# Attention, routed experts and an MLP on one core: scatters, slots and the masks of the block factors in another order

## The chip, the core and the metric

The kernel runs on one core of a Trainium2 chip. The core has five engines with a queue of instructions each, executed in the order of the program: TensorE (PE) for matmuls, VectorE (DVE), ScalarE (ACT), GpSimd (POOL) and SyncE (SP), which here only issues transfers. The metric is the time of one execution on the device in microseconds (us).

## The reference

Three layers follow each other. The first is a recurrent attention with gates, over 4 batches, 8 heads, 768 tokens and a head width of 40; the second sends each of the 3072 tokens to one of 8 experts; the third is a gated MLP.

```python
for t in range(S):                                  # attention
    m_new = max(f_gate[t] + m, i_gate[t])
    f_stab, i_stab = exp(f_gate[t] + m - m_new), exp(i_gate[t] - m_new)
    C = f_stab * C + i_stab * outer(v[t], k[t])
    n = f_stab * n + i_stab * k[t]
    y[t] = sigmoid(o_gate[t]) * (C @ q[t]) / max(abs(n @ q[t]), 1)
...
idx = argmax(norm(x) @ norm(expert_emb).T / tau)    # experts
out[idx == e] = gate * (relu(x[idx == e] @ w1[e]) @ w2[e])
...
h = x @ w_in                                        # MLP
return (h * sigmoid(1.702 * h)) @ w_out
```

## The kernel before

The attention works in 24 units, one for each batch and each chunk of 128 tokens, chunk by chunk: unit u is batch u mod 4 of chunk u // 4. One loop (`for u in range(0, NU - 1)`) writes out by hand what stands where: inside `tc.manual_schedule()` every engine gets its instructions in the order of the text, so an instruction that waits holds all behind it on its engine. Iteration u holds pieces of several units at once:

- TensorE: `scores_mm(u)` (sp, L483), `route_rank` every fourth time (L668 to L672), `pv(u - 1)` (op, L546), `route_t(u - 2)` (the transposes pr of x, L590 to L592), `state(u)` (dC, L497), `inter(u)` (ip, L533), `far_mm(u + 1)` (tri, L439), `route_l(u - 2)` (the router's products, L621 to L623, into a PSUM bank r that is there once).
- VectorE: `state_up(u - 1)` (Cst, L518), `epilogue1` (num, L558), `scan(u + 1)` (tri from fb, L427; pmb, L431, in the first two chunks), `route_slot` (L689, L691), `scores_w(u)` (wm, L488), halves of expert weights (L110, L111, L121), `epilogue2` (L565 to L574), the copy of the router's result out of bank r (logit_all, L625), `route_hot` (L643 to L651) and `route_cnt` (L680, L681) for four tiles at a time.
- ScalarE: the copy of the scan's half block (pmb, L429), `rk_all` (L674), the ones of vp_in (L464), xT (L594), the sigmoid (L552), the squares (L600), `state_decay(u)` (L504) and `far_out(u + 1)` (pmb, L444).
- GpSimd: `finish(u - 2)` (sg, L581, and x, L584), `vprime(u + 1)` (vp_in, L463), `kweigh(u + 1)` (kw, L470), and from iteration 10 on `scatter` (L699), an indirect transfer that puts one tile of x into the experts' rows, with a small memset behind it.
- SyncE: the loads of k, q, v and of the decays fb for later units, and of expert weights.

From chunk 2 on (unit 8 and later) the decays of a chunk between its two halves are a product of two factors. `factors` makes fb in iteration 4. `suffix` makes facA on VectorE in two parts (L360, iterations 5 and 6), and its second part also casts it to fa on ScalarE (L364) and subtracts on VectorE (L366). `spread_b` makes eight masked copies of fb on ScalarE (rhsB, L382), `spread_a` four of fa (lhsA, L378); `far_mm` multiplies them, and `far_out` copies the result into pmb. In iteration 6 two tiles are routed, 3 and 4, one after the other. The slots that `route_slot` finds are what the scatters of the tiles need; `route_hot` runs at the end of iterations 6, 9, 13, 17 and 21, rank and slots in the next.

Of the kernel before, what the change touches and what calls it, by code (L numbers as in the profile page):

```python
# [26 lines left out]
def kernel(ctx, tc, qT_in, kT_in, kvo_in, i_gate, f_gate, expert_emb, tau, w12, wio, out, dbg=None):  # L27

    nc = tc.nc
    B, H, S = i_gate.shape  # L30
# [110 lines left out]
    with ExitStack() as actx:  # L141
# [11 lines left out]
        R3, HP, CH = 3 * BH, P // 2, 2  # L153
# [16 lines left out]
        units = [(b, c) for c in range(NCH) for b in range(B)]  # L170
# [182 lines left out]
        def suffix(second):  # L353

            if not second:
                nc.gpsimd.memset(facA[:, :, HP - 1:HP], 1.0)
                nc.gpsimd.tensor_copy(facA[:, :, 0:HP - 1], fz[:, CH:NCH, 1:HP])
            k = 8 if second else 1
            while k < (HP if second else 8):
                nc.vector.tensor_tensor(out=facA[:, :, 0:HP - k], in0=facA[:, :, 0:HP - k], in1=facA[:, :, k:HP], op=ALU.mult)  # L360
                k *= 2
            if not second:
                return
            nc.scalar.copy(fac["fa"], facA)  # L364
            lo = slice(BH, 2 * BH)
            nc.vector.tensor_tensor(out=fac["fa"][lo], in0=facA[lo], in1=fac["fa"][lo].bitcast(F32), op=ALU.subtract)  # L366
# [75 lines left out]
        def far_out(u):  # L442
            if units[u][1] >= CH:
                nc.scalar.copy(pm[u][:, :, HP:P], tri_t.pop(u))  # L444
# [21 lines left out]
        def kweigh(u, eng=nc.gpsimd):  # L466
            if units[u][1] == NCH - 1:
                return
            kw[u] = wk.tile([P, H, D], F32, tag="kw", name="kw")
            eng.tensor_tensor(out=kw[u], in0=kvo[u][:, 0],  # L470
                                    in1=pm[u][:, :, P - 1:P].to_broadcast([P, H, D]), op=ALU.mult)
# [13 lines left out]
        def scores_w(u):  # L485
            wm[u] = wk.tile([P, H, P], F32, tag="wm", name="wm")
            for hs, sp in sp_t.pop(u):
                nc.vector.tensor_tensor(out=wm[u][:, hs], in0=sp, in1=pm[u][:, hs], op=ALU.mult)  # L488
# [173 lines left out]
        def route_rank(us, late=None):  # L662

            oh, old, new = hot[us[0]]
            rp = r_bank(late)
            n = len(us)
            rk = rp[:, 0:n * E].rearrange("p (n e) -> p n e", e=E)
            nc.tensor.matmul(rk, ones16, base16.unsqueeze(1).to_broadcast([P, n, E]), start=True, stop=False)  # L668
            nc.tensor.matmul(rk, ones16, old.unsqueeze(1).to_broadcast([P, n, E]), start=False, stop=False)
            for i in range(n - 1):  # L670
                nc.tensor.matmul(rk[:, i + 1:n], ones16, oh[:, i:i + 1].to_broadcast([P, n - 1 - i, E]), start=False, stop=False)
            nc.tensor.matmul(rk, tri16, oh, start=False, stop=True)  # L672
            if late is None:
                nc.scalar.copy(rk_all[:, tile_ids(us)], rk)  # L674
            rp_t[us[0]] = rk
# [7 lines left out]
        def route_slot(us, late=False):  # L683
            n = len(us)
            oh, old, new = hot[us[0]]
            rk = rp_t.pop(us[0])
            tis = tile_ids(us)
            sl_ = wk.tile([P, n, E], F32, tag="sl_", name="sl_")
            nc.vector.tensor_tensor(out=sl_, in0=rk, in1=oh, op=ALU.mult)  # L689
            with nc.allow_low_precision(reason="whole numbers, one of them not zero"):  # L690
                nc.vector.tensor_reduce(out=slot_i[:, tis], in_=sl_, axis=AX.X, op=ALU.add)  # L691
            if late:
                nc.vector.tensor_copy(rk_all[:, tis], rk)
# [183 lines left out]
        with tc.manual_schedule():  # L877
# [34 lines left out]
            for u in range(0, NU - 1):  # L912
                if ok(u - 4):
                    finish(u - 2, nc.gpsimd)
                if ok(u + 2):
                    fload(u + 2)
                if u == 3:
                    finish(1, nc.gpsimd)
                if u > 1:
                    scores_mm(u)  # L920
                if u > 1:
                    state_up(u - 1)
                if ok(u - 1):
                    epilogue1(u - 1)
                if u == 1:
                    state(0)
                    scores_w(1)
                    state_up(0)
                if u in (2, 5):
                    scores_w(u)  # L930
                if u and ok(u + 1):
                    scan(u + 1)
                if batch:
                    route_rank(batch)
                    route_slot(batch)
                    pend.extend(batch)
                if u not in (0, 1, 2, 5):
                    scores_w(u)
                if u == 2:
                    norm_en2()  # L940
                if u == 4:
                    gates_z(2, NCH)
                if 0 <= u - 1 - W0 < WH:
                    split_half_lo(u - 1 - W0)
                if u == 0:
                    scan(1)
                    gates_m(2, NCH)
                if ok(u - 1):
                    pv(u - 1)
                    epilogue2(u - 1)  # L950
                if u == 5:
                    gates_pe(2, NCH)
                if u in (5, 6):
                    suffix(u == 6)
                if u == 1:
                    masks()
                if ok(u + 1):
                    vprime(u + 1)
                    if units[u + 1][1] < CH:
                        kweigh(u + 1)  # L960
                if u == 3:
                    gates_x(2, NCH)
                if u == 4:
                    put_dec(1)
                    gates_exp_i(2, NCH)
                rts = {2: [], 3: [0], 4: [1], 5: [2], 6: [3, 4]}.get(u, [u - 2] if ok(u - 2) else [])
                if rts:
                    route_t(rts[0])
                if u == NU - 2:
                    inter(u + 1, True)  # L970
                if u > 4:
                    sigm(u)
                elif u < 2:
                    sigm(u + 1)
                if u == 4:
                    order_consts()
                if u == 2:
                    finish(0, nc.gpsimd)
                if u:
                    state(u)  # L980
                if u == 3:
                    prep_en()
                if len(rts) > 1:
                    route_t(rts[1])
                    route_l(rts[0])
                inter(u)
                if ok(u + 1):
                    far_mm(u + 1)
                for i in rts[-1:]:
                    route_l(i)  # L990
                for i in rts:
                    route_sq(i)
                    if i % B == B - 1:
                        newb = [i - j for j in range(B - 1, -1, -1)]
                        route_hot(newb)
                if batch:
                    route_cnt(batch)
                batch, newb = newb, None
                state_decay(u)
                if ok(u + 1) and units[u + 1][1] >= CH:  # L1000
                    far_out(u + 1)
                    kweigh(u + 1)
                if u in (5, 6):
                    spread_b(H // 2 * (u - 5), H // 2 * (u - 4))
                if u == 6:
                    spread_a()
                if u == 3:
                    sigm(u)
                    gates_exp_f(2, NCH)
                    gates_xi(2, NCH)  # L1010
                if u == 4:
                    gates_e(2, NCH)
                    sigm(u)
                for i in range(0 if u < US else 1 if u < NU - 5 else 2):
                    if pend:
                        scatter(pend.pop(0))
                if ok(u + 3):
                    load_k(u + 3)
                    load_q(u + 3)
                    load_v(u + 3)  # L1020
                if 0 <= u - Z0 < NZ:
                    zero_slots(u - Z0)
                if u == W0 - 2:
                    first()
                if u == W0 - 1:
                    ids[0] = nc.values_load(first_i, engines=[mybir.EngineType.SP], min_val=0, max_val=E - 1)
                if u in WLOAD:
                    load_w(WLOAD.index(u))
                if 0 <= u - W0 < WH:
                    split_half(u - W0)  # L1030
# [697 lines left out]
```

## Time and profile before

| | us |
|---|---|
| median of 3 runs (768.67 to 770.9) | 770.32 |
| the profiled execution | 769.16 |
| its span, first to last instruction | 767.5 |

Busy time of the engines by stretch of the span, in us, with the granted TensorE clock and the share of the DMA engines:

| stretch | TensorE | VectorE | ScalarE | GpSimd | clock | DMA |
|---|---|---|---|---|---|---|
| 0 to 74, attention, first two chunks | 52.73 | 59.87 | 32.71 | 35.10 | 0.91 | 0.72 |
| 74 to 211, attention, other chunks, end of it | 118.62 | 110.45 | 65.98 | 82.72 | 1.00 | 0.61 |
| 211 to 405, experts | 191.72 | 171.04 | 124.00 | 74.40 | 1.00 | 0.72 |
| 405 to 767.5, MLP | 353.01 | 188.29 | 144.67 | 38.53 | 0.99 | 0.14 |

A busy time is a sum over a stretch and does not tell which engine the others wait for; that is read from the rows of the waits and from the instructions in order of time. A clock of 1.00 is the full TensorE clock of 2.4 GHz, 0.50 its lower level of 1.2 GHz.

### The profile page before, as it was taken

The page shows a single profiled execution, that of the slowest core. Times are in us where ns is not written, and L with a number is a line of the kernel's source. Part 1 is how long each engine was busy: PE and PEld are TensorE (multiplying, and loading weights), DVE is VectorE, ACT ScalarE, POOL GpSimd, SP SyncE. Part 2 cuts the span into 40 slices and gives each one's busy share as a digit, 9 for nine tenths or more (in the row PEclk, how much of TensorE's full clock was granted, in tenths as well). Part 3 has the DMA queues.
Part 4 walks back from the last instruction along what each step waited for, and adds up shares of the span by engine and source line. Part 5 has one row for each costly group of instructions (what it writes and reads, how often), then busy time and mean ns, then how long its engine had stood idle before and what let it go on. Part 6 is the DMA issues. An engine that isn't in the chain of part 4 may idle for free.

```text
span 767.5 us, 13326 instructions
## 1 busy us (share of the span) xinstructions
PE 716.1 (93%) x4724; PEld 672.3 (88%) x4724; DVE 529.6 (69%) x1095; ACT 367.4 (48%) x852; POOL 230.8 (30%) x348
## 2 busy tenths in 40 slices
PE   7695988888889999999999999999999999999995
PEld 6595887888789999999999988998898889889994
DVE  7896888788569899898986764554554554445542
ACT  4354454553456666576655443343343343334442
POOL 4462456577424333364511003003003002002011
PEclk9997999999999999999999999999999999999998
DMA  6984866673268776867853121110111111101000
GB/s 188 309 254 152 261 213 195 170 236 129 88 233 208 208 220 204 193 206 238 251 143 101 22 62 35 37 47 35 36 48 35 32 31 36 43 1 44 13 18 18
DMA packets 70490, 95.78 MB, mean 125 GB/s; under 512 B 31794, under 2 KB 56530, under 8 KB 70418
## 3 DMA queue, kind: packets, MB, share of 16 engines
q1 hardware_dynamic: 67346, 86.99, 39.2%
q0 software_dynamic: 3072, 7.89, 2.8%
q8 instruction: 38, 0.62, 0.3%
q14 instruction: 34, 0.28, 0.1%
HBM read 73.73 MB, written 17.19 MB: 118 GB/s over the span
## 4 chain that ended last, share of the span: by engine, by line
issue 41%; PE 23%; POOL 5%; DVE 2%; DMA 1%; POOLq 0%; ACT 0%; SPq 0%; ACTq 0%
PE acc L1228 11%; PE hp L138 10%; POOL out_dram L1273 3%; POOL xr L1379 2%; PE xt L1152 1%; DMA xr<-y 1%; DVE w L121 0%; POOL gap L1275 0%; DVE hs L1202 0%; DVE xl L1154 0%; DVE w L111 0%; DVE fr L1297 0%; POOLq L1723 0%; DVE xl L1170 0%; PE xt L1168 0%
## 5 line engine op out<-in xcount | busy, mean ns | idle before, releaser
L1228 PE MATMUL acc<-wout,hhl 128*128 128x320 f32 x1152 | 187.0, 309 | 0.0
L1228 PEld LDWEIGHTS acc<-wout,hhl 128*128 128x128 f32 x1152 | 175.9, 188 | 7.4
L1213 DVE TENSOR_TENSOR sg<-hp,sg 128x512 f32<-128x512 f32 (+1 forms) x112 | 68.9, 615 | 93.5 <-ACT sg L1212 86.8
L138 PE MATMUL hp<-xh,win 128*128 128x512 f32 (+1 forms) x560 | 131.0, 364 | 0.0
L1212 ACT ACTIVATE sg<-hp 128x512 f32<-128x512 f32 (+1 forms) x112 | 60.4, 539 | 124.5 <-PE hp L138 124.0
L1215 DVE TENSOR_TENSOR hhl<-sg,hhl 128x512 fp32r<-128x512 f32 (+1 forms) x112 | 71.4, 637 | 70.3 <-ACT hhl L1214 69.8
L1273 POOL DMA_INDIRECT out_dram<-o,tokd x24 | 24.1, 1002 | 312.2 <-ACT o L1257 308.6
L1228 PE MATMUL acc<-w,hs 128*128 128x320 f32 x636 | 104.9, 310 | 2.0 <-ACT hs L1201 1.0
L138 PEld LDWEIGHTS hp<-xh,win 128*128 128x128 f32 x560 | 93.9, 188 | 11.5 <-ACT xh L1418 0.2
L1214 ACT CAST hhl<-sg 128x512 fp32r<-128x512 f32 (+1 forms) x112 | 62.7, 560 | 80.2 <-DVE sg L1213 75.9
L1228 PEld LDWEIGHTS acc<-w,hs 128*128 128x128 f32 x636 | 96.8, 188 | 4.5 <-DVE hs L1202 1.9
L138 PE MATMUL hp<-xl,win 128*128 128x512 f32 (+1 forms) x336 | 85.7, 363 | 0.0
L110 POOL TENSOR_TENSOR w<-r,w 128x256 fp32r<-128x256 f32 x58 | 47.7, 823 | 106.6 <-ACT w L105 90.4
L138 PEld LDWEIGHTS hp<-xl,win 128*128 128x128 f32 x336 | 58.8, 189 | 10.9 <-DVE xl L1419 0.2
L138 PE MATMUL hp<-xh,w 128*128 128x440 f32 (+6 forms) x320 | 66.8, 338 | 0.0
L483 PE MATMUL sp<-qT,kblk 120*128 120x128 f32 x384 | 50.7, 289 | 4.1 <-DVE wm L488 4.1
L138 PEld LDWEIGHTS hp<-xh,w 128*128 128x128 f32 x320 | 51.4, 189 | 1.7
L483 PEld LDWEIGHTS sp<-qT,kblk 120*128 120x128 f32 x384 | 48.5, 205 | 5.0 <-DVE wm L488 4.5
L1201 ACT ACTIVATE hs<-hp 128x440 fp32r<-128x440 f32 (+6 forms) x64 | 30.3, 473 | 41.6 <-PE hp L138 38.7
L546 PE MATMUL op<-vp_in,wm 128*128 128x96 f32 (+1 forms) x368 | 44.2, 273 | 0.1
L546 PEld LDWEIGHTS op<-vp_in,wm 128*128 128x128 f32 x368 | 42.9, 192 | 0.3 <-DVE num L565 0.3
L138 PE MATMUL hp<-xl,w 128*128 128x440 f32 (+6 forms) x192 | 42.9, 331 | 0.0
(324 smaller groups left out, 1126.4 us busy)
## 6 DMA issues: line engine op xcount, KB each, us to landing
r<-in_w_dram SPq DMA_DIRECT2D x32, 704.0 KB
kvo<-in_kvo_dram SPq DMA_DIRECT2D x24, 480.0 KB
c<-in_wio_dram SPq DMA_DIRECT2D x16, 704.0 KB
rows<-zt SPq DMA_DIRECT2D x8, 640.0 KB
qT<-in_qT_dram SPq DMA_DIRECT2D x24, 180.0 KB
fb<-dec SPq DMA_DIRECT2D x32, 128.0 KB
fb<-dec SPq DMA_DIRECT2D x7, 512.0 KB
xr<-y SPq DMA_DIRECT2D x5, 640.0 KB
```

The source lines that it names most:

```text
L110: eng.tensor_tensor(out=t[:, 3 * P:5 * P].rearrange("p (c f) -> p c f", c=2), in0=r1[:, 0:2], in1=hif[:, 0:2], op=ALU.subtract)
L138: nc.tensor.matmul(hp, a, b, start=(i == 0), stop=(i == len(seq) - 1))
L483: nc.tensor.matmul(sp[:, h - hs.start], kblk[u % NLD][0:KR, h // 3, h % 3, :], qT[u][0:KR, h // 3, :], start=True, stop=True)
L546: nc.tensor.matmul(ops[:, h * NW:h * NW + n], wm[u][:, h], vp_in[u % NLD][:, h * DV:h * DV + n], start=True, stop=True)
L1201: nc.scalar.activation(out=hh, in_=hp, func=AF.Relu)
L1212: nc.scalar.activation(out=sg, in_=hp, func=AF.Sigmoid, scale=1.702)
L1213: nc.vector.tensor_tensor(out=g, in0=hp, in1=sg, op=ALU.mult)
L1214: nc.scalar.copy(hh, g)
L1215: nc.vector.tensor_tensor(out=hl, in0=g, in1=hh.bitcast(F32), op=ALU.subtract)
L1228: nc.tensor.matmul(acc_t[blk][i], hl if j == 2 else hh, w[:, DM:2 * DM] if j == 1 else w[:, 0:DM], start=(first and j == 0), stop=(last an ...
L1273: sc = nc.gpsimd.indirect_dma_start(out=out, out_offset=bass.IndirectOffsetOnAxis(ap=tokd[:, ti:ti + 1], axis=0), in_=o[:, i], in_offset=None)
L1379: eng.tensor_tensor(out=xr_t[blk], in0=xr_t[blk], in1=gated[:, t0:t0 + n].unsqueeze(2).to_broadcast([P, n, 3 * P]), op=ALU.mult)
```

## The change

Three things in the unit loop are written in another order; no operation is added or left out. `suffix` no longer holds the cast of facA to fa and the subtraction: a new function `factor_a` holds them and is called in iteration 6 behind the decay of the state, ahead of `spread_a`. `spread_b` makes all eight copies in iteration 5 instead of four in 5 and four in 6. The scatters stand ahead of `far_out` and `kweigh`, so on GpSimd ahead of the weighing of the keys (`far_out` is ScalarE's and keeps its place there). And `route_slot` stands behind `scores_w`.

```diff
             while k < (HP if second else 8):
                 nc.vector.tensor_tensor(out=facA[:, :, 0:HP - k], in0=facA[:, :, 0:HP - k], in1=facA[:, :, k:HP], op=ALU.mult)
                 k *= 2
-            if not second:
-                return
+
+        def factor_a():
             nc.scalar.copy(fac["fa"], facA)
             lo = slice(BH, 2 * BH)
             nc.vector.tensor_tensor(out=fac["fa"][lo], in0=facA[lo], in1=fac["fa"][lo].bitcast(F32), op=ALU.subtract)
...
                 if batch:
                     route_rank(batch)
+                if u not in (0, 1, 2, 5):
+                    scores_w(u)
+                if batch:
                     route_slot(batch)
                     pend.extend(batch)
-                if u not in (0, 1, 2, 5):
-                    scores_w(u)
...
                 state_decay(u)
-                if ok(u + 1) and units[u + 1][1] >= CH:
-                    far_out(u + 1)
-                    kweigh(u + 1)
-                if u in (5, 6):
-                    spread_b(H // 2 * (u - 5), H // 2 * (u - 4))
-                if u == 6:
-                    spread_a()
...
                 for i in range(0 if u < US else 1 if u < NU - 5 else 2):
                     if pend:
                         scatter(pend.pop(0))
+                if ok(u + 1) and units[u + 1][1] >= CH:
+                    far_out(u + 1)
+                    kweigh(u + 1)
+                if u == 5:
+                    spread_b(0, H)
+                if u == 6:
+                    factor_a()
+                    spread_a()
```

ScalarE from the end of iteration 5 to the end of iteration 6, before (rhsB and lhsA are the masked copies, xT the router's input, sg a sigmoid, sq squares, Cst the state):

```order
L382 ACTIVATE rhsB<-fb,hmask 96x4x64 x4
L364 CAST fa<-facA 96x256
L464 COPY vp_in_123<-ei_tok 128x8
L594 COPY xT<-pr 128x384
L552 ACTIVATE sg<-kvo 128x320
L594 COPY xT<-pr 128x384
L600 ACTIVATE sq,ss_all<-x 128x320 x2
L504 ACTIVATE Cst_190<-Cst_190,gdec 120x123 x3
L382 ACTIVATE rhsB<-fb,hmask 96x4x64 x4
L378 ACTIVATE lhsA<-fa,bmask 96x256 x4
```

The same place on ScalarE after the change:

```order
L382 ACTIVATE rhsB<-fb,hmask 96x4x64 x8
L464 COPY vp_in_123<-ei_tok 128x8
L594 COPY xT<-pr 128x384
L552 ACTIVATE sg<-kvo 128x320
L594 COPY xT<-pr 128x384
L600 ACTIVATE sq,ss_all<-x 128x320 x2
L504 ACTIVATE Cst_190<-Cst_190,gdec 120x123 x3
L364 CAST fa<-facA 96x256
L378 ACTIVATE lhsA<-fa,bmask 96x256 x4
```

The cast has moved from ahead of both xT to behind the decay, and the second four copies of fb from behind the decay to ahead of xT.

VectorE at the end of iteration 6 and in iteration 7, where the subtraction L366 and the slots (sl_, slot_i) change places with their neighbours:

```order
 L649 TENSOR_REDUCE mx<-vv 128x4
 L651 TENSOR_TENSOR oh_all<-vv,mx 128x4x8
+L366 TENSOR_TENSOR fa<-facA,fa 32x256
 L518 SCALAR_TENSOR_TENSOR Cst_190<-dC,mask_178,Cst_190 120x3x41 x3
 L558 TENSOR_TENSOR num<-ip,ei_tok 128x328
 L427 SCALAR_TENSOR_TENSOR tri<-fb,id_132 128x512
-L689 TENSOR_TENSOR sl__840<-r,oh_all 128x32
-L691 TENSOR_REDUCE slot_i<-sl__840 128x4
 L488 TENSOR_TENSOR wm<-sp,pmb_141 128x1024
+L689 TENSOR_TENSOR sl__842<-r,oh_all 128x32
+L691 TENSOR_REDUCE slot_i<-sl__842 128x4
 L565 TENSOR_TENSOR num<-num,op 128x328
```

The subtraction now stands between the routing and the state's update, no longer directly behind facA's products, and the slots stand behind the weighing of the scores.

GpSimd in one of the iterations 10 to 18, before:

```order
L584 TENSOR_TENSOR x<-num,sg 128x320
L463 TENSOR_TENSOR vp_in_122<-kvo,ei_tok 128x8x40
L470 TENSOR_TENSOR kw<-kvo,pmb_141 128x320
L699 DMA rows<-x,slot_i 26624x320
L701 MEMSET gap 1x1
L581 TENSOR_TENSOR sg<-sg,dn 128x320
L584 TENSOR_TENSOR x<-num,sg 128x320
```

The same on GpSimd after the change:

```order
L584 TENSOR_TENSOR x<-num,sg 128x320
L463 TENSOR_TENSOR vp_in_122<-kvo,ei_tok 128x8x40
L699 DMA rows<-x,slot_i 26624x320
L701 MEMSET gap 1x1
L470 TENSOR_TENSOR kw<-kvo,pmb_141 128x320
L581 TENSOR_TENSOR sg<-sg,dn 128x320
L584 TENSOR_TENSOR x<-num,sg 128x320
```

The scatter and its memset have moved from between kw and sg to between vp_in and kw. From iteration 19 on no keys are weighed, and the order there is the same as before.

## Rows read from the trace of the kernel before

**Rows 1.** Windows: stretch, its length, busy us (instructions), granted clock, DMA share, GB/s.

```profile
60.80:67.20 6.40, 0.02 (x1) 0.00 (x0) 5.65 (x10) 0.90 (x4) 2.99 (x4) 0.63 0.12 28
67.20:73.70 6.50, 6.47 (x34) 6.47 (x35) 2.22 (x11) 6.07 (x17) 0.00 (x0) 0.58 0.37 98
73.70:80.00 6.30, 6.30 (x63) 6.24 (x63) 5.40 (x17) 3.41 (x12) 1.06 (x2) 1.00 0.77 250
```

**Rows 2.** Timeline, ScalarE: start, us, what; in brackets idle before it and releaser.

```profile
53.83 1.69 ACT L382 ACTIVATE rhsB<-fb,hmask 96x256 fp32r<-96x256 f32 x4
66.30 0.41 ACT L364 CAST fa<-facA 96x256 fp32r<-96x256 f32 x1 [10.78 <-DVE facA L360]
...
66.71 0.47 ACT L594 COPY xT<-pr 128x384 f32<-128x384 f32 x1
```

**Rows 3.** Timeline, VectorE, iterations 6 and 7.

```profile
64.23 1.98 DVE L360 TENSOR_TENSOR facA<-facA 96x224 f32<-96x224 f32 x3
66.73 0.41 DVE L366 TENSOR_TENSOR fa<-facA,fa 32x256 fp32r<-32x256 f32 x1 [0.53 <-ACT fa L364]
...
71.48 0.17 DVE L625 COPY logit_all<-r 128x8 f32<-128x8 f32 x1 [2.39 <-PE r L623]
...
72.68 0.85 DVE L518 SCALAR_TENSOR_TENSOR Cst<-dC,mask,Cst 120x123 f32<-120x123 f32 x3
```

**Rows 4.** Timeline, TensorE, iterations 6 and 7.

```profile
57.79 0.27 PE L592 MATMUL pr<-ident,x 128*128 128x128 f32 x1
...
67.23 0.80 PE L621 MATMUL r<-enT,xT 128*128 128x128 f32 x2 [6.41 <-ACT xT L594]
...
69.88 0.71 PE L621 MATMUL r<-enT,xT 128*128 128x128 f32 x2
...
71.23 2.66 PE L483 MATMUL sp<-qT,kblk 120*128 120x128 f32 x16
```

**Rows 5.** Waits from 55 to 190 us: who for whom, us in total, times, longest.

```profile
POOL kw L470 <- ACT pmb L444: 42.9, 12, 12.2
...
PE pr L590 <- POOL x L584: 12.4, 11, 1.7
```

**Rows 6.** Timeline, GpSimd: an x, four steps in a row, another scatter.

```profile
80.44 1.60 POOL L584 TENSOR_TENSOR x<-num,sg 128x320 f32<-128x320 f32 x1
...
114.37 0.74 POOL L470 TENSOR_TENSOR kw<-kvo,pmb 128x320 f32<-128x320 f32 x1 [2.66 <-ACT pmb L444]
115.27 1.82 POOL L699 DMA_INDIRECT rows<-x,slot_i  x1 [0.16 <-issue]
...
117.14 0.73 POOL L581 TENSOR_TENSOR sg<-sg,dn 128x320 f32<-128x320 f32 x1
117.95 0.88 POOL L584 TENSOR_TENSOR x<-num,sg 128x320 f32<-128x320 f32 x1
...
123.06 1.01 POOL L699 DMA_INDIRECT rows<-x,slot_i  x1 [0.15 <-issue]
```

**Rows 7.** Timeline, VectorE: two scans, and one of the five first slots.

```profile
79.95 1.50 DVE L427 TENSOR_TENSOR_SCAN tri<-fb,id 128x512 f32<-128x512 f32 x1
...
115.05 1.22 DVE L427 TENSOR_TENSOR_SCAN tri<-fb,id 128x512 f32<-128x512 f32 x1
...
126.69 0.19 DVE L689 TENSOR_TENSOR sl__1467<-r,oh_all 128x32 f32<-128x32 f32 x1 [0.73 <-ACT rk_all L674]
```

**Rows 8.** Timeline, TensorE, iterations 13 to 15: scores and the transposes behind them.

```profile
113.60 1.95 PE L483 MATMUL sp<-qT,kblk 120*128 120x128 f32 x16
...
118.88 0.33 PE L590 MATMUL pr<-ident,x 128*128 128x128 f32 x1 [1.60 <-POOL x L584]
...
121.41 1.95 PE L483 MATMUL sp<-qT,kblk 120*128 120x128 f32 x16
...
126.61 0.33 PE L590 MATMUL pr<-ident,x 128*128 128x128 f32 x1 [1.08 <-POOL x L584]
...
133.79 0.33 PE L590 MATMUL pr<-ident,x 128*128 128x128 f32 x1 [0.98 <-POOL x L584]
```

## The prediction

> **What bounds the kernel now.** The change sits in the loop over 24 units (iteration u) of the attention, so I first cut the trace into stretches. In each the reader should look at TensorE's busy time and at its granted clock. Around 61 to 67 us TensorE does next to nothing, and after that it works at a mean granted clock of 0.58, which is mostly the lower of its two levels (1.2 instead of 2.4 GHz): 34 matmuls in 6.5 us, against 63 in the 6.3 us that follow [rows 1]. That is one stall. To see what ends it I read ScalarE, VectorE and TensorE in order of time there [rows 2 to 4]. ScalarE stands 10.78 us at the cast of facA into fa (L364), because the products that make facA (L360) are late on VectorE, from 64.23 to 66.21. Behind the cast, in program order, stands the copy xT (L594), and TensorE waits 6.41 us for it.
>
> From iteration 11 to 19 there is a second loss, found in the list of waits: TensorE's transposes of x (pr, L590) wait for GpSimd's x (L584), 12.4 us in 11 waits, while GpSimd itself waits 42.9 us for pmb before it weighs keys (kw, L470) [rows 5]. GpSimd's order there is kw, scatter, sg, x [rows 6]: the scatter lies on the way from pmb to x, though it needs nothing from kw. TensorE's unit shows it: scores start at 113.60, pr at 118.88 after 1.60 us of waiting, the next scores at 121.41 [rows 8]. So 7.81 us a unit, 6.21 without the wait. In this stretch TensorE's own work is the floor, and x is what it waits for.
>
> **Part 1: the cast of fa and the masked copies.** The order on ScalarE after the change is: eight masked copies of fb at the end of iteration 5, then xT, xT, squares, decay, and only then the cast. The eight copies take twice the 1.69 us of four [rows 2], from 53.83 to 57.2. They are hidden: ScalarE was idle there until 66.30, and the first pr that it copies is finished at 58.06 [rows 4]. So the first xT (0.47 us) ends at about 58.6 instead of 67.18, and route_l of the first tile (L621) and the state's matmuls run by some 62.5 us instead of from 67.23 on.
>
> Then a new wait takes the place of the old. Both route_l write the same PSUM bank r, so the second needs VectorE's copy of the first (L625), and that copy stands in VectorE's queue behind facA's products. Until 66.21 it cannot start; with it at 66.21 to 66.4, the second route_l starts at 66.4 instead of 69.88 [rows 4]. From that start to the second copy L625 it was 71.48 - 69.88 = 1.60 us [rows 3, 4], so the copy comes at 68.0 instead of 71.48: 3.5 us sooner. The routing steps up to Cst (L518) were 72.68 - 71.48 = 1.20 us, and now the subtraction L366 (0.41 us, before it lay in a pause) stands there too: 68.0 + 1.20 + 0.41 = 69.6 against 72.68, **3.1 us** [rows 3]. TensorE's scores of unit 7 would come at 66.4 + (71.23 - 69.88) = 67.75, 3.5 us sooner; VectorE is the later one, so 3.1 counts. Behind the cast ScalarE has only the masked copies of fa, as long as four of fb, 1.69 us; they wait for L366 at 69.6 and end at 71.3, and the copy of tri behind them has to wait for the next scan anyway. SyncE's loads of q wait for the state's matmuls and go out sooner, at a time when hardly any DMA runs (a share of 0.12 [rows 1]).
>
> Bounds: TensorE now pauses some 4 us instead of 6.4, and I expect the clock to fall all the same. If the low clock lasts as long after the pause as it did, it covers half a unit more of pv than before: 2.5 us. If the clock does not fall or is back sooner, the scores are 0.7 us shorter (2.66 against 1.95 us [rows 4, 8]) and the second route_l by about 0.4: 4.2 us. I take 3.1, which leaves the clock as the rows show it.
>
> **Part 2: the scatter ahead of kw.** In iterations 10 to 18 the scatter now fills GpSimd's wait for pmb. It starts behind vp and takes 1.01 to 1.82 us [rows 6] of a wait that was 2.8 us on the mean without the longest ((42.9 - 12.2) / 11) [rows 5], so kw starts when it did. The nine pr of iterations 11 to 19 lose their scatter. Their waits are all of [rows 5] less two small ones, 11.5 us: that is the ceiling.
>
> But the scatter also met something: VectorE's scan (L427, 1.22 us) began at 115.05 and ended at 116.27 [rows 7], and the scatter beside it took 1.82 us, clear of it 1.01; an x that met the scan of 79.95 took 1.60 against 0.88 [rows 6, 7]. Now sg meets it. In iteration 13, kw ends at 115.11. If the scan holds sg until 116.27, sg ends at 117.0 (0.73), x at 117.95 (0.88 and 0.08 between), pr at 118.0 instead of 118.88: 0.87 us. If sg goes first, the scan follows and x is the long one: 115.84 + 0.08 + 1.60 = 117.52, pr at 117.57: 1.31 us. I take 1.05 for the four iterations of this kind (12, 13, 16, 17): 4.2 us. In 14 and 18 VectorE first does the routing, the scan comes later than sg and x, and the wait of 1.08 [rows 8] goes altogether: 2.15 us. In 11, 15 and 19 VectorE comes late out of the slots, its late scan holds ScalarE's copy of tri and with it xT, pmb and kw; the wait there is 0.98 [rows 8]. I take 0.2 each, 0.6, between -0.1 and 0.98. Sum 4.2 + 2.15 + 0.6 = **6.9 us**; bounds 4 x 0.87 + 2 x 0.5 - 0.3 = 4.2 and 4 x 1.31 + 2.15 + 2.95 = 10.3.
>
> The Trainium skill, page "SBUF — State Buffer", section "SBUF: two separate sides", has a rule that speaks against this part: VectorE and GpSimd share one pair of ports under an exclusive lock, a VectorE instruction with two SBUF inputs takes it against a GpSimd instruction that reads SBUF, and whoever comes second waits for the whole of the other. By it the scatter was partly paying a lock that somebody has to pay, and the four iterations give about 1 us each; without it they would give their full waits of 1.6 and the sum would be 9 us. The 1.82 and 1.60 us of the trace agree with the rule.
>
> **Part 3: slots behind the weighing of scores.** The slots (L689) waited 0.73 us for ScalarE's rk_all in each of five iterations [rows 7], and the weighing (L488) behind them; now the weighing goes first and covers that wait. VectorE gains 3.6 us in all. I cost it at nothing: TensorE waits for x, not for VectorE, and the sum of part 2 already lets VectorE run close behind. The slots read bank r later, which the next route_l needs; by the spacing above it is free just in time. Bounds: 0.3 us lost to 0.7 gained in each, within the range of part 2.
>
> **Sum.** 3.1 + 6.9 = 10.0 us; the sum of the bounds is 6.7 to 14.5. Nothing behind the attention waits on a fixed time: the experts and the second MLP follow TensorE. The profiled execution took 769.16 us, so 759.2; the median of the runs shown is 1.16 us above it, so I predict **760.3 us**, its own range 755.8 to 763.6.
>
> **Rivals.** (1) VectorE takes over. Its lateness passes through scan, tri, xT, pmb and kw into x. Then 11, 15 and 19 lose 0.5 us each, the four gain 0.5 each and 14 and 18 gain 0.6: 1.7 instead of 6.9, with part 1 together 4.8, so 765.5. For it speaks that VectorE has little slack left after slots; against, that part 3 gives it 0.73 us just there. (2) The scan does not meet sg and all nine waits go: 3.1 + 11.5 = 14.6, so 755.7. For it speaks the 6.21 us of TensorE; against, the 1.60 us x. (3) The scatter's place gives nothing, because xT becomes the later input: part 1 alone, 767.2; half of this case is a part 1 so small that no change can be told. (4) Slower: the low clock stays. TensorE's pause is cut in two, with the state's matmuls in the middle, and if the clock falls later and then does not come back, a unit of 6.2 us takes 6.2 x 63/34 = 11.5 [rows 1], 5.3 more. From two such units it eats the 10 us, three give 776. Against it speaks that after the pause TensorE has more to do without a break than before, and that the clock came back there.
>
> **How the numbers follow.** Forecast 0.60, rival 1 0.16, rival 2 0.08, rival 3 0.10, rival 4 0.06. The range goes from rival 2 to rival 1, 755.5 to 766.0, and leaves out rivals 3 and 4. A measurement tells about 0.3% (2.3 us) from no change: faster 0.60 + 0.16 + 0.08 + half of 0.10 = 0.89, same 0.05, slower 0.06.
>
> **What would show it.** Part 1: ScalarE's wait of 10.78 us at the cast is gone or harmless, xT at about 58.6, TensorE waiting for L625 until about 66.4, scores of unit 7 at 67.5 to 68. Part 2: the scatter between vp and kw, TensorE's waits for x down from 12.4 to about 5 us, long sg or x (1.5 us) beside the scan, units of 6.7 instead of 7.8 us. Part 3: no wait for rk_all. It is wrong if kw starts later behind the scatter, if TensorE then waits for xT or for bank r, or if the clock stays low past 72 us.

## The result and the profile after

The changed kernel took **757.52 us** (median of 4 runs, 756.38 to 759.28), the kernel before beside it 770.09 us: a ratio of 0.984, 95% interval 0.982 to 0.987. It was measured twice more, on two chips on which the kernel before took 766.78 and 766.77 us: 756.38 (ratio 0.987, 0.985 to 0.989) and 755.92 (0.986, 0.984 to 0.987). So the gain is 12.6 us in the first measurement and 10.4 and 10.9 in the later two; forecast were 10.0.

**Part 1 in the trace.** ScalarE around iteration 6, by start, duration, engine, line and what ended the idle time, against [rows 2]:

```profile
52.97 3.29 ACT L382 ACTIVATE rhsB<-fb,hmask 96x256 fp32r<-96x256 f32 x8
57.23 0.48 ACT L594 COPY xT<-pr 128x384 f32<-128x384 f32 x1 [0.89 <-PE pr L592]
...
65.38 0.40 ACT L364 CAST fa<-facA 96x256 fp32r<-96x256 f32 x1 [2.87 <-DVE facA L360]
```

The eight masked copies lie in one piece. xT is copied at 57.23, 9.5 us sooner than before, and the wait at the cast has gone from 10.78 us to 2.87, with nothing behind it for which TensorE then waits. The new wait is where it was forecast. TensorE, VectorE, and the time on either side of the pause (columns of the last: stretch in us; its length; busy time and instructions of TensorE, of its weight load, of VectorE, ScalarE and GpSimd; granted clock; DMA share; GB/s):

```profile
60.46 0.80 PE L533 MATMUL ip<-Cst,qT 120*128 120x123 f32 x6
65.57 0.46 PE L621 MATMUL r<-enT,xT 128*128 128x128 f32 x2 [4.31 <-DVE logit_all L625]
```
```profile
63.37 1.97 DVE L360 TENSOR_TENSOR facA<-facA 96x224 f32<-96x224 f32 x3
65.27 0.15 DVE L625 COPY logit_all<-r 128x8 f32<-128x8 f32 x1
```
```profile
61.30:65.50 4.20, 0.00 (x0) 0.00 (x0) 3.95 (x9) 1.33 (x6) 2.56 (x4) 1.00 0.71 208
65.50:71.60 6.10, 6.03 (x44) 6.00 (x45) 4.89 (x14) 2.75 (x8) 0.43 (x1) 0.72 0.47 148
71.60:77.70 6.10, 6.10 (x57) 6.02 (x55) 4.63 (x16) 2.91 (x9) 2.74 (x3) 1.00 0.53 158
```

The copy of the first logits stands behind facA's products in VectorE's queue, so the second round starts at 65.57 instead of 69.88 [rows 4]. Against [rows 1], TensorE does 44 matmuls in the 6.1 us behind the pause, at 0.72, where it did 34 at 0.58.

**Part 2 in the trace.** GpSimd in iteration 12 to 13, against [rows 6]:

```profile
105.68 1.07 POOL L699 DMA_INDIRECT rows<-x,slot_i  x1 [0.16 <-issue]
...
108.19 0.74 POOL L470 TENSOR_TENSOR kw<-kvo,pmb 128x320 f32<-128x320 f32 x1 [1.35 <-ACT pmb L444]
108.89 1.71 POOL L581 TENSOR_TENSOR sg<-sg,dn 128x320 f32<-128x320 f32 x1
110.67 0.81 POOL L584 TENSOR_TENSOR x<-num,sg 128x320 f32<-128x320 f32 x1
```

VectorE's scan beside it, and the same operations (scan, sg, x) one iteration earlier:

```profile
102.69 1.56 DVE L427 TENSOR_TENSOR_SCAN tri<-fb,id 128x512 f32<-128x512 f32 x1 [0.18 <-DMA fb<-dec]
102.44 0.72 POOL L581 TENSOR_TENSOR sg<-sg,dn 128x320 f32<-128x320 f32 x1
103.24 1.60 POOL L584 TENSOR_TENSOR x<-num,sg 128x320 f32<-128x320 f32 x1
...
108.86 1.22 DVE L427 TENSOR_TENSOR_SCAN tri<-fb,id 128x512 f32<-128x512 f32 x1
```

The scatter now lies inside the wait for pmb. What it met there, sg and x meet instead: sg takes 1.71 us beside a scan of 1.22, or, where sg comes first (at 102.44, 0.72 us), scan and x stretch to 1.56 and 1.60. Both cases that the forecast spoke of occur. The Trainium skill, page "SBUF — State Buffer", section "SBUF: two separate sides", has whoever comes second in the pair of ports shared by VectorE and GpSimd wait for the whole of the other. Here 1.71 us is the scan's rest of 1.19 (108.86 + 1.22 less 108.89) and about half a us, where a wait for the whole and then sg's 0.72 would make 1.91. So the rule's direction holds here, with some overlap. The list of waits, 50 to 180 us, against [rows 5] (who for whom, us in total, times, longest):

```profile
POOL kw L470 <- ACT pmb L444: 30.2, 12, 9.0
...
PE r L621 <- DVE logit_all L625: 4.3, 1, 4.3
PE pr L590 <- POOL x L584: 4.2, 9, 0.8
```

TensorE's wait for x fell from 12.4 us to 4.2 (forecast: about 5). No wait for rk_all is left.

**By stretches.** The starts of scores (L483, TensorE) cut the attention into units. Three stretches serve for all that follows: scores 6 to 8 (part 1), 11 to 20 (part 2), 20 to 23 (the last units).

| kernel | 6 to 8 | 11 to 20 | 20 to 23 |
|---|---|---|---|
| before | 24.47 | 68.31 | 19.11 |
| after, first measurement | 21.27 | 60.70 | 19.57 |
| after, measured again (e8_after, e9_after) | 21.87, 21.85 | 60.66, 60.95 | 19.53, 18.90 |

Of the 11.56 us between the two first profiled executions (769.16 and 757.6), 3.20 lie in the first stretch, 7.61 in the second, -0.46 in the third; 0.87 more stands at scores 6 already, ahead of anything that the change moves. Taken by its places, the forecast of 3.1 and 6.9 looks right. The experiments show that this is not all of it.

### The profile page after: what moved, and what is told of

The parts are those of the page before. It is cut to its first block, busy times and chain, and to the rows that moved or that the text cites. A ratio compares the mean times of both kernels' runs of the same rounds, so it can differ in the third digit from the quotient of the medians.

```text
span 755.9 us, 13328 instructions
## 1 busy us (share of the span) xinstructions
PE 714.8 (95%) x4724; PEld 671.3 (89%) x4724; DVE 527.7 (70%) x1095; ACT 367.3 (49%) x852; POOL 234.3 (31%) x348
## 4 chain that ended last, share of the span: by engine, by line
issue 41%; PE 24%; POOL 5%; DVE 1%; DMA 1%; POOLq 0%; ACT 0%; SPq 0%; ACTq 0%
PE acc L1230 12%; PE hp L138 11%; POOL out_dram L1275 3%; POOL xr L1381 2%; PE xt L1154 1%; DMA xr<-y 1%; POOL gap L1277 0%; DVE w L121 0%; POOLq L1725 0%; DVE xl L1172 0%; PE xt L1170 0%; DVE hs L1204 0%; DVE xl L1156 0%; DVE w L111 0%; ACT w L118 0%
## 5 line engine op out<-in xcount | busy, mean ns | idle before, releaser
L138 PEld LDWEIGHTS hp<-xl,win 128*128 128x128 f32 x336 | 58.8, 189 | 10.9 <-DVE xl L1421 0.2
L483 PE MATMUL sp<-qT,kblk 120*128 120x128 f32 x384 | 50.7, 289 | 2.6 <-DVE wm L488 2.6
L483 PEld LDWEIGHTS sp<-qT,kblk 120*128 120x128 f32 x384 | 48.2, 204 | 3.4 <-DVE wm L488 2.8
```

The costliest lines, as they stand in the source:

```text
L138: nc.tensor.matmul(hp, a, b, start=(i == 0), stop=(i == len(seq) - 1))
L483: nc.tensor.matmul(sp[:, h - hs.start], kblk[u % NLD][0:KR, h // 3, h % 3, :], qT[u][0:KR, h // 3, :], start=True, stop=True)
```

## The experiments

The experiments ran in three groups of four kernels (e1 to e4, e5 to e8, e9 to e12), each group on a chip of its own, with the kernel before timed beside it (766.88, 766.78, 766.77 us). Where two kernels of different groups are compared, the text says so.

**Each part alone, and parts 1 and 2 without 3.** e1_cast has part 1 alone: the cast of fa and its masked copies behind the state's decay (`factor_a` as in the change), and all of spread_b in iteration 5:

```diff
-                if u in (5, 6):
-                    spread_b(H // 2 * (u - 5), H // 2 * (u - 4))
+                if u == 5:
+                    spread_b(0, H)
                 if u == 6:
+                    factor_a()
                     spread_a()
```

> Only part 1 on the kernel before: the cast of fa and its subtraction behind the decay of iteration 6, all eight masked copies of fb in iteration 5. My theory: the three parts work in different stretches and add up. From the scores of unit 6 to those of unit 8 it was 24.47 us before and 21.27 with all three parts; part 1 alone gives this whole 3.2 us, and the units from 10 to 20 stay at 68.3 us: 770.1 - 3.2 = 766.9. Rival: the low clock eats part 1 (the scores of unit 7 took 3.48 us in the changed kernel), so in another execution it gives between 2 and 4: 766 to 768. If it gives less than 1, the 3.2 came from elsewhere.

e2_scatter moves only far_out and kweigh behind the scatters:

```diff
-                if ok(u + 1) and units[u + 1][1] >= CH:
-                    far_out(u + 1)
-                    kweigh(u + 1)
...
                     if pend:
                         scatter(pend.pop(0))
+                if ok(u + 1) and units[u + 1][1] >= CH:
+                    far_out(u + 1)
+                    kweigh(u + 1)
```

> Only part 2 on the kernel before: scatters ahead of the weighing of the keys. My theory: this is the larger half. From the scores of unit 11 to those of unit 20 it was 68.31 us before and 60.70 with all parts; part 2 alone gives 6 to 7.6 of it: 762.5 to 764. Waits of TensorE for x go from 12.4 us to about 4 to 6, and sg or x beside the scan are long (1.6 to 1.7 us). Rival: the slots in the old place make VectorE too late in iterations 10, 14 and 18, and part 2 without part 3 gives 5 or less: 765 or more. Other rival, no lock: all of 11.5 us, 758.6.

e3_slots moves only the slots:

```diff
                 if batch:
                     route_rank(batch)
+                if u not in (0, 1, 2, 5):
+                    scores_w(u)
+                if batch:
                     route_slot(batch)
                     pend.extend(batch)
-                if u not in (0, 1, 2, 5):
-                    scores_w(u)
```

> Only part 3 on the kernel before: the slots behind the weighing of the scores. My theory: nothing, 770.1 within 1 us, since TensorE waits for GpSimd's x, which does not depend on VectorE there; the five waits of 0.73 us for rk_all go. Rival: VectorE is already in the way, and the 3.6 us that it saves come out as 1.5 to 3.6: 766.5 to 768.6.

e4_no_slots is the changed kernel with that last edit undone.

> The changed kernel with the slots in their old place (parts 1 and 2 without 3). My theory, as I now read the trace after: with the scatters out of the way VectorE is close behind TensorE, so the slots are worth something there: iterations 11, 15 and 19 get longer by about 0.5 us each, 759.0 instead of 757.5. If parts simply add and part 3 is worth nothing: 757.5. If part 3 made the scatters work in the first place: over 761.

| kernel | median us | ratio to before, 95% | 6 to 8 | 11 to 20 | 20 to 23 |
|---|---|---|---|---|---|
| e1_cast | 764.33 | 0.995 (0.993 to 0.998) | 22.59 | 73.88 | 18.77 |
| e2_scatter | 759.20 | 0.990 (0.987 to 0.994) | 23.94 | 60.67 | 23.19 |
| e3_slots | 767.60 | 1.001 (0.999 to 1.003) | 24.65 | 68.56 | 20.15 |
| e4_no_slots | 759.16 | 0.989 (0.986 to 0.992) | 21.32 | 60.61 | 22.72 |

Part 1 alone gains 2.6 us by the medians, part 2 alone 7.7, part 3 alone nothing. (The 73.88 us of e1_cast come of its profiled execution, at 769.09 us the slowest of 12 runs with a median of 764.33: at 116 to 120 us its granted clock was 0.57, and three more such stretches follow.) Parts 1 and 2 work where they should: 21.3 in the first stretch, 60.6 in the second. But together they stay 2.8 us short of the changed kernel (759.16 against 756.38, of different groups), and both kernels that have the new scatters and the old slots lose 3 to 4 us between scores 20 and 23.

**Is part 3 worth something beside the others?** The changed kernel and the kernel without part 3 once more, side by side (e8_after, of the second group, is the changed kernel too).

> The changed kernel itself, on the same chip as the three that follow. Its ratio to the kernel before was 0.984; the two parts tried alone gave 3.5 and 7.5 us against a kernel before of 766.9, 11.0 together, which gives 755.9 here. If part 3 (the slots behind the weighing) pays beside parts 1 and 2, this kernel comes out at 755 to 756, some 3 us under the 759.2 of the kernel with parts 1 and 2 alone; if it pays nothing, at 758 to 759.

> The changed kernel once more, on the same chip as the three that follow, for their comparison: 756 to 757.5 against a kernel before of 767 to 770.

> Parts 1 and 2 without part 3, a second time, now on the same chip as the changed kernel. Their first comparison went over two calls and left 2.8 us between them (759.2 and 756.4), with intervals that overlap. If part 3 pays beside the others: again 2 to 3 us above the changed kernel. If it pays nothing, as it did alone: within 1 us of it. In the trace of its first run the loop from scores 11 to scores 20 was as fast as the changed kernel's (60.6 us), and all that it lost lay behind scores 22 (11.3 us to the next against 8.8), where the granted clock was 0.50 for 4 us; if that belongs to the order, the stretch has the low clock again, if it is a matter of the single execution, it need not.

e8_after: 756.38. e9_after: 755.92, ratio 0.986 (0.984 to 0.987). e10_no_slots: 759.35, ratio 0.990 (0.988 to 0.991). Part 3 is worth 3.4 us beside parts 1 and 2: the slowest run of e9_after took 756.45 us, the fastest of e10_no_slots 757.17. TensorE in iteration 22 and 23 of e9_after and of e10_no_slots:

```profile
170.49 0.22 PE L671 MATMUL r<-oh_all,ones 128*128 128x24 bf16 x3 [0.86 <-DVE oh_all L651]
...
172.41 0.28 PE L590 MATMUL pr<-ident,x 128*128 128x128 f32 x1
...
173.47 1.57 PE L533 MATMUL ip<-Cst,qT 120*128 120x123 f32 x12 [0.57 <-ACT xT L594]
```
```profile
171.69 0.22 PE L671 MATMUL r<-oh_all,ones 128*128 128x24 bf16 x3 [1.59 <-DVE oh_all L651]
...
173.79 0.42 PE L590 MATMUL pr<-ident,x 128*128 128x128 f32 x1
...
175.20 2.86 PE L533 MATMUL ip<-Cst,qT 120*128 120x123 f32 x12 [0.57 <-ACT xT L594]
```

The same matmuls, at half the pace. The two at 172 to 180 us (columns as above):

```profile
172.00:175.00 3.00, 2.43 (x22) 2.19 (x21) 2.86 (x9) 2.04 (x7) 2.10 (x4) 1.00 0.13 55
175.00:180.00 5.00, 5.00 (x47) 4.96 (x46) 3.82 (x10) 1.13 (x3) 3.14 (x6) 1.00 0.32 131
```
```profile
172.00:175.00 3.00, 2.63 (x19) 2.23 (x18) 2.24 (x5) 1.10 (x4) 1.24 (x3) 0.73 0.17 58
175.00:180.00 5.00, 4.80 (x22) 4.71 (x23) 2.12 (x8) 1.93 (x6) 3.78 (x8) 0.50 0.27 110
```

In 5 us TensorE does 22 matmuls at a granted clock of 0.50 (1.2 GHz), against 47 at 1.00. This low stretch is in all three traces with the new scatters and the old slots (e2_scatter, e4_no_slots, e10_no_slots) and in none of the three of the changed kernel. It lasts some 6.7 us in each of the three. Of the 3.96 us that e10_no_slots takes longer than e9_after from scores 20 to 23, 3.33 lie in the last unit, with the low clock, and 0.54 in the first, at 1.00. So the traces put most of part 3's gain in TensorE's clock behind the last routing. Why the clock falls in the one order is not shown. The pauses are nearly alike: 1.59 and 0.57 us here; the first trace of the changed kernel has 1.52 and 0.57 at the same place and keeps 1.00.

**Is x still the bound behind the change?** e5_finish lets GpSimd finish unit u-1 ahead of the keys instead of behind them:

```diff
-                if ok(u - 4):
+                if 0 <= u - 4 and u < 8:
                     finish(u - 2, nc.gpsimd)
...
+                if 7 <= u < NU - 2:
+                    finish(u - 1, nc.gpsimd)
                 if ok(u + 1) and units[u + 1][1] >= CH:
```

> The changed kernel, with GpSimd's finish (sg and x) of unit u-1 issued at the end of iteration u, ahead of the weighing of the keys, in iterations 7 to 21; before, it was at the top of the next iteration, behind the keys. Theory: in the changed kernel the loop still waits for GpSimd, because the keys wait for ScalarE's copy of the masks (30.2 us in 12 waits) and x stands behind them; TensorE's wait for x (4.2 us in 9 waits) goes, the loop from scores 11 to scores 20 falls from 60.7 us to 57 to 59, and the time falls by 2 to 4 us. Rival: the loop is at VectorE's pace already (scan, weighing and numerators), and the scan now meets the keys or x in the shared port pair instead: 60.5 us for the loop, no change in the time; and it gets slower by 1 to 3 us if the keys, now later, hold TensorE's state.

It took 752.54 us, 3.8 less than e8_after beside it (ratio to before 0.982, 0.980 to 0.984). Its slowest run, 753.37, lies under the fastest of e8_after, 755.92. The wait of TensorE for x is gone from the list, and so is GpSimd's for ScalarE's copy pmb (L444); GpSimd now waits for dn, which it needs for sg:

```profile
POOL sg L581 <- DVE dn L574: 29.7, 15, 7.4
```

The stretch 11 to 20 takes 56.94 us against 60.66. So the changed kernel still waited for x, for pmb's sake: kw needs pmb, and sg and x stood behind kw although they need nothing of it, as the scatter had stood there before.

**Is it VectorE's queue that holds TensorE in iteration 6?** e6_products gives the three second products of facA to GpSimd, behind its keys:

```diff
-                if u in (5, 6):
-                    suffix(u == 6)
+                if u == 5:
+                    suffix(False)
...
                     kweigh(u + 1)
+                if u == 6:
+                    suffix(True, nc.gpsimd)
```

> The changed kernel, with the second round of the gates' products (facA, three operations of 1.97 us in VectorE's queue in iteration 6) on GpSimd, behind its weighing of the keys. Theory: in the changed kernel these products hold the second copy of logits on VectorE and so TensorE's second round of logits (waits 4.3 us in iteration 6); without them scores of unit 7 start 2 to 4 us earlier, and the interval from scores 6 to scores 8 falls from 21.3 us to 17.5 to 19.5. Rival: ScalarE's masked copies (1.7 us behind the last product) become the bound since GpSimd takes longer for the same products: 21 us or more, and the time stays or rises by up to 2 us.

It took 754.10 us, 2.3 less than e8_after (ratio to before 0.985, 0.982 to 0.987; the runs of the two overlap, 753.41 to 757.4 against 755.92 to 756.7). TensorE's wait there, and GpSimd's products:

```profile
66.38 0.76 PE L621 MATMUL r<-enT,xT 128*128 128x128 f32 x2 [2.65 <-DVE logit_all L625]
```
```profile
64.59 1.87 POOL L360 TENSOR_TENSOR facA<-facA 96x224 f32<-96x224 f32 x3
```

4.31 us became 2.65: less by 1.66, the greater part of the products' 1.97. The rest of the wait is VectorE's weighing and denominators ahead of that copy. Scores 6 to 8 took 19.44 us against 21.87, at the upper end of what was expected. Of these 2.43 us, 1.68 lie ahead of scores 7, as much as the wait lost; 0.75 lie behind, where the low clock ended at 69 us and not at 71.

**Does the low clock come of the pause?** e12_warm fills the 4.3 us with matmuls of the identity, whose result nothing reads:

```diff
+                if u == 6:
+                    keep_warm(ps_t.tile([P, G, P], F32, tag="pt", name="pr").rearrange("p a t -> p (a t)"), 34)
                 for i in rts[-1:]:
                     route_l(i)
```

> The changed kernel, with 34 matmuls of 128x128 of the identity into a spare bank ahead of the second round of logits in iteration 6, in the 4.3 us in which TensorE waits for VectorE's copy of the first; their result is not used. If the low clock behind that pause (0.50 from 67 to 69 us, the 16 scores of unit 7 in 3.48 us) comes of the pause: the stretch from 65.5 to 71.6 has the granted clock 1.00, the scores take 1.95 us, the interval from scores 6 to scores 8 falls from 21.3 to 19 to 20 us, and the time by 1 to 2 us. If it comes of something else, the clock falls as before and nothing changes. If the matmuls last longer than the wait, the interval grows by what they overhang.

TensorE's timeline and the granted clock in that kernel:

```profile
61.06 7.79 PE L84 MATMUL pr<-ident 128*128 128x128 f32 x68
68.69 0.39 PE L621 MATMUL r<-enT,xT 128*128 128x128 f32 x2
...
69.36 1.95 PE L483 MATMUL sp<-qT,kblk 120*128 120x128 f32 x16
```
```profile
65.50:69.00 3.50, 3.50 (x34) 3.50 (x33) 0.00 (x0) 0.27 (x1) 0.41 (x1) 1.00 0.57 198
69.00:75.70 6.70, 6.70 (x66) 6.53 (x65) 5.83 (x18) 3.78 (x12) 0.00 (x0) 1.00 0.09 27
```

On the clock its one trace answers yes: without the pause it stays at 1.00 from 56 to 78 us, the scores of unit 7 take 1.95 us, and scores 7 to 8 take 6.33 us against 7.73 in e9_after. As a version it fails: 760.73 us, 4.8 more than e9_after (ratio to before 0.993, 0.991 to 0.996). I had sized the filling wrongly. 34 matmuls are 68 rows, two for each, and took 7.79 us, so TensorE came back 3.1 us late (68.69 against 65.57 in the first trace of the changed kernel), more than the clock gives. That accounts for 1.0 us from scores 6 to 8 (22.87 against 21.85 in e9_after); 0.7 more stands from scores 8 to 11. Another 1.7 us of the profiled execution lies at a later branch, where TensorE waited 2.1 us for its own sequencer and in e9_after 0.4; why, and where the remainder is, stays open.

**Both edits together, and part 3 inside that version.** e7_both has the edits of e5_finish and e6_products on the changed kernel. e11_both_old is the same with the slots back ahead of the weighing.

> The two edits together on the changed kernel. If both theories hold their gains add: 4 to 7 us under the changed kernel. If either falls, this has the other's gain alone.

> The version with both edits that gained 6.6 us over the changed kernel (GpSimd's finish ahead of the keys, the second round of products on GpSimd), with the slots back in their old place ahead of the weighing of scores. In that version GpSimd's and TensorE's waits for x are gone and VectorE's 55.4 of 60 us are nearly the pace of the loop, so a wait of VectorE for the copy of the ranks (0.7 us in five iterations before) would now stand on the path. If it does: 752 to 754. If part 3 pays nothing here either: 749 to 750.5.

e7_both: **749.75 us**, ratio to before 0.979 (0.977 to 0.981), 6.6 us less than the changed kernel beside it. The gains add (3.8 and 2.3 make 6.1). From 100 to 160 us, of the changed kernel and of e7_both:

```profile
100.00:160.00 60.00, 56.22 (x497) 54.32 (x496) 54.05 (x131) 33.01 (x101) 44.86 (x56) 1.00 0.75 227
```
```profile
100.00:160.00 60.00, 59.87 (x525) 57.05 (x525) 55.37 (x132) 33.81 (x105) 48.48 (x62) 1.00 0.79 235
```

TensorE is busy for 59.87 of 60 us: here its own work is the bound. e11_both_old, of the next group: 753.85 us, ratio 0.983 (0.981 to 0.985), 4.1 us more than e7_both; the two intervals touch. In the traces the loss lies in the loop itself, 59.29 us from scores 11 to 20 against 56.30, at a granted clock of 1.00 in both, with waits that e7_both does not have:

```profile
DVE sl__1467 L689 <- ACT rk_all L674: 0.7, 1, 0.7
DVE sl__1818 L689 <- ACT rk_all L674: 0.7, 1, 0.7
```

These two are 1.4 of the 3 us; TensorE now has waits of 0.2 to 0.8 us for pmb, kw and oh_all, and how these make up the rest is open. So in the loop part 3 is worth nothing where TensorE waits for x anyway, and some 3 us where nothing else is late.

## Why the prediction was right, and where its steps were not

The time lay inside the range and inside the forecast's own range, 2.8 us under the forecast. Of these 2.8, 0.8 lie in parts 1 and 2 themselves (3.20 and 7.61 for 3.1 and 6.9) and 0.9 ahead of scores 6, which the change does not touch; 1.2 come of carrying over that the median lies 1.16 us above the profiled execution, where after the change it lies 0.08 below; the rest nearly cancels. Two terms of the sum held, one failed, and an effect that was not in the sum hid it.

**Part 1, 3.1 us: right.** The traces of the changed kernel give 2.6 to 3.2 between scores 6 and 8, e1_cast 2.6 by the medians and 1.9 in its trace. The steps up to the pause came as told, 0.87 us earlier as the whole iteration was: masked copies in one piece, the first xT done at 57.7, TensorE waiting for L625 until 65.6, a low clock behind the pause all the same. The last step did not: the forecast took VectorE for the later one and counted its 3.1. But TensorE, back at work at 65.57, has no wait before 78 us in the trace. Scores of unit 7 came 4.05 us sooner by the distance from scores 6 (3.39 in the two later traces), and 0.85 (0.79 and 0.77) were given back at the next, where the 16 scores ran at the low clock (3.48 us, before 2.66). So 3.20 is TensorE's gain less the clock's price, and that it is close to VectorE's 3.1 is luck.

**Part 2, 6.9 us: right, slightly low.** The traces give 7.4 to 7.6 in the stretch of scores 11 to 20. The four iterations costed at 1.05 each gave 1.15 to 1.43 (0.56 to 1.80 in e9_after): the price of meeting the scan is shared by GpSimd and VectorE as told, and smaller than told. The forecast had its 1.82 and 1.60 us agree with the rule of an exclusive lock; a wait for the rest of the scan (1.00 and 1.01 us) and then the time alone (1.01 and 0.88) would have made 2.01 and 1.89 of them, so there too the rule held only in part. Iterations 14 and 18 gave 0.78 instead of 1.08, because TensorE now waits 0.30 us for oh_all there; the three costed at 0.2 gave 0.69, 0.19 and 0.19. Of the rivals, VectorE did not take over (rival 1), nor did all waits go (rival 2): 4.2 us for x were left, and they are gone in e5_finish.

**Part 3, nothing: wrong by 3.4 us.** The argument was that TensorE waits for x and not for VectorE. As an argument on the loop it was right: with the slots in their old place the loop took 60.6 to 60.8 us, as with the new. What it left out is that the order on VectorE could matter behind the loop: in the traces the gain lies after the last routing, most of it in TensorE's clock, where the forecast had looked at nothing.

**The sum's silence on what follows scores 20: wrong by 3 to 4 us the other way.** I had let everything behind the loop follow TensorE unchanged. With parts 1 and 2 alone the low clock appears there, so that the two, forecast at 10.0, gave 7.4 (766.77 to 759.35) and 7.7. This is close to rival 4, a low clock behind a cut-up pause, in another place and, in the traces, only with the new scatters and without part 3; rival 4 had it eat all 10 us, and here it took 3 to 4. Since part 3 takes it away, the two errors cancel in the changed kernel, and that a forecast made of the parts came out right as a sum is luck.

How firm this is: the 3.4 us between e10_no_slots and e9_after are a comparison of timed runs side by side. That they lie in the clock at 173 to 180 us rests on one profiled execution of each kernel, three of them with the low stretch. The profiled executions of e4_no_slots and e10_no_slots took 760.42 and 760.19 us, each the slowest of its kernel and about 1 us above the median, and that of e2_scatter 762.15, 3 us above; so their other runs may have less of it.

## What to carry to other kernels

When a step on an in-order queue is moved out of the way, look at what now stands behind the same wait: the scatter stood behind kw without need, and so did sg and x, for another 3.8 us. A reordering that covers a wait on an engine with slack gave nothing in this loop, and some 3 us once the other bounds were gone, so try it again after each other gain. Price the end of a loop apart from its middle, and read the granted clock there: a sum over iterations does not contain it.

## What the runs showed of the hardware

The granted clock was the largest thing outside the sum. With the pause of iteration 6 (1.0 to 6.4 us) every trace has one or two stretches at 0.50 between 59 and 74 us, of some 3 to 10 us; in the one trace with the pause filled there was none. Where it begins differs for one and the same kernel: in e8_after and e9_after inside the pause, at 64 us, in the first trace of the changed kernel only when TensorE was back at work, at 66, after a pause at 1.00 throughout.

The length of a pause alone does not tell whether the clock falls. In iteration 22, pauses of 1.59 or 1.60 us and 0.57 us were followed by a low stretch in three traces; in the eleven others, with a first pause of 0.23 to 1.52 us, there was none. But a pause of 1.63 us stands ahead of the state's matmuls (L497) in iteration 6 of nearly every trace. In the first trace of the changed kernel and in e4_no_slots, with the windows behind it:

```profile
58.83 0.80 PE L497 MATMUL dC<-vp_in,kw 128*120 128x123 f32 x6 [1.63 <-DVE Cst L518]
60.65 0.88 PE L497 MATMUL dC<-vp_in,kw 128*120 128x123 f32 x6 [1.63 <-DVE Cst L518]
```
```profile
58.80:61.10 2.30, 2.27 (x21) 2.30 (x21) 2.30 (x2) 0.96 (x4) 0.00 (x0) 1.00 0.59 191
60.60:64.40 3.80, 3.75 (x21) 3.79 (x21) 3.80 (x4) 1.97 (x7) 0.74 (x1) 0.58 0.41 125
```

The clock stays at 1.00 in the one; in the other it is 0.58 over the window, 0.50 from 61.5 us on. It falls so, ahead of the next pause, in e4_no_slots, e5_finish and e11_both_old, and in no other trace. What else decides is open.
